# Group 3's queries and keys turned by the crossbar, with the output weights loaded behind two groups' rows

## The chip, the core and the metric

The kernel runs on one core of a Trainium2 chip. The metric is the time of one execution on the device in microseconds, as the median of several runs. The core has five engines with queues of their own: TensorE (PE, matrix products; PEld is its weight load), VectorE (DVE), ScalarE (ACT), GpSimd (POOL) and SyncE (SP). Here POOL issues all loads that change the type from float32 to bfloat16, SP issues the crossbar transposes and most stores, and ACT issues a few stores. An engine works through its queue in order, and an instruction that waits holds everything behind it on that engine.

## What is computed

Windowed attention with a few sink positions, and behind it a gated feed-forward block on the joined heads.

```python
B, H, S, D = 4, 8, 768, 64;  n_sink, window = 4, 128
scores = (q @ k.T) / sqrt(D)                  # by batch and head
keep = (col < n_sink) | ((row - col >= 0) & (row - col < window))
a = softmax(where(keep, scores, -1e9))
x = (a @ v).transpose(0, 2, 1, 3).reshape(3072, 512)
g = x @ w_gate                                # 512 x 1536
out = (g * sigmoid(g) * (x @ w_val)) @ w_out  # w_out: 1536 x 512
```

## The kernel before

**Groups and blocks.** Attention goes by groups of 256 tokens, three to a batch: group 0 to 2 are batch 0, group 3 to 5 batch 1, and so on to group 11. The feed-forward block goes by token blocks of `SIZES` = 256, 256, 256, 512, 512, 512, 512, 256. Block 3 takes groups 3 and 4, block 4 groups 5 and 6.

**The steps of a group.** `load_nat` (L106) loads the group's rows of k and q, four loads of 128 KB, into a tile `nat`. The rows must be turned, so that the head's dimension lies across the partitions: the tiles `kT` and `qT`. There are two ways. `step_TN` (L273) turns 128 tokens of k or q with four PE transposes into one PSUM bank (`pn`, L279), and ACT or DVE copies the bank out (L283, L285). `xbar` (L287) has SP issue four crossbar transposes (L293), straight from `nat` into `kT` and `qT`. Before the change group 2 and group 3 go by `step_TN`, and groups 4 to 11 by `xbar`. Then come:

- `step_S1`, `step_S2`, `step_S3`: the scores on PE (L382), the exponentials on ACT (L395), and the products with the mask on DVE (L404). `step_S1` also takes the scores of the sinks (`mm_K`, L432).
- `step_PV` (L469): the product with v on PE (L454 and L463 for sinks and neighbours, L494), and the division by the sum on DVE (L503, L511) into `xn`.
- `step_X` (L523): `xn` is turned into the feed-forward input `xT`, for groups above 2 by two crossbar transposes on SP (L538).

`load_v` loads v, for the first group of a batch as `va` (L151), for the others as parts of `vm` (L128).

**The feed-forward steps.** A gate unit (`gate`) makes one PSUM bank each of x times `w_gate` (`pg`) and x times `w_val` (`pv`), both at L564, with a tanh on ACT (L584) and two DVE operations (L592 and L598 to L607) into `ht`. An output unit (`down`, L644) multiplies 128 tokens of `ht` with the four tiles `wo` of the output weights, twelve matmuls of 512 columns (L657), copies the bank out on ACT (L662) and stores it (L665). Three matmuls use each tile `wo`.

**The order.** It is written out by hand. The list `us` holds the units of the feed-forward block, and `weave` runs them in turn; `slots` gives each unit the attention steps that are put into it. In the first list, units 0 to 3 belong to blocks 0 and 1, units 4 to 11 to both, units 12 to 17 are the gate units of block 2, and units 18 to 23 are six output units, two for each of the blocks 0, 1 and 2. In an output unit the steps are spread evenly between its twelve matmuls:

```python
for i, a in enumerate(attn):
    at.setdefault(DFC * (i + 1) // (len(attn) + 1), []).append(a)
```

A step marked `ahead` runs before a gate unit's first product. In the second list block 3 starts, whose first two units need the turned results of group 3 and whose next two those of group 4; group 5's scores stand in its second unit.

**The loads.** Before the first list, POOL's queue gets all weights and the rows and v of groups 2 and 3 in the order of the code: gate weights 1 and 2, rows of group 2, gate weights 3, v of group 2, gate weights 4 and 5, four output weights (`load_out`), rows of group 3, v of group 3. Rows and v of group 4 follow. POOL's loads take turns on eight semaphores, and each load waits until the load eight places before it has landed. SP's and ACT's transfers share eight others in the same way. `vcl` holds the sinks' v of batches 1 to 3: POOL clears it, and SP loads eight small pieces into it.

**Buffers.** The pool `rowp` has three buffers under the tag `rows`: two first hold the staged rows of group 0, one those of group 1, and then `nat` of groups 2 and 3 take one each. From group 4 on `nat` has one buffer of its own in `natp`, so that the rows of a group wait for the transposes of the group before. PSUM has eight banks for everything (`bank`).

Of the kernel before, what the change touches and what calls it, by code (L numbers as in the profile page):

```python
# [8 lines left out]
BF16 = mybir.dt.bfloat16  # L9
# [5 lines left out]
def kernel(  # L15
# [12 lines left out]
    nc = tc.nc  # L28
    P = 128
# [3 lines left out]
    DM = moe_w_gate.shape[0]  # L33
# [21 lines left out]
    def pool(name, bufs, psum=False):  # L55
        if psum:
            return ctx.enter_context(
                tc.tile_pool(name=name, bufs=bufs, space=bass.MemoryType.PSUM))
        return ctx.enter_context(tc.tile_pool(name=name, bufs=bufs))

    const = pool("const", 1)
    wpool = pool("wpool", 1)
    rowp = pool("rowp", 3)
    natp = pool("natp", 1)
# [19 lines left out]
    rows, nats, vas = {}, {}, {}  # L84
# [20 lines left out]

    def load_nat(g):  # L106
        b, c = divmod(g, GC)
        x = (natp if g > 3 else rowp).tile(
            [P, 2, 2, DM], BF16, tag="nat" if g > 3 else "rows", name="nat")
        for i, src in ((0, k), (1, q)):  # L110
            for j in range(2):
                t0 = c * 256 + j * P
                nc.gpsimd.dma_start(  # L113
                    x[:, i, j].rearrange("p (h d) -> p h d", d=D),
                    src[b, :, t0:t0 + P].rearrange("h p d -> p h d"))
        nats[g] = x
# [3 lines left out]
    def load_vm(g):  # L120

        b, c = divmod(g, GC)
        if b not in vms:
            vms[b] = vpool.tile([P, 6, H, VS], BF16, tag=f"vm{b}", name="vm")
            nc.gpsimd.memset(vms[b][:, :, :, D:D + 1], 1.0)

        def part(t, p0, p1, t0):
            nc.gpsimd.dma_start(  # L128
                vms[b][p0:p1, t - 1, :, 0:D],
                v[b, :, t0:t0 + p1 - p0].rearrange("h p d -> p h d"))  # L130

        T = 2 * c
        if g - 1 not in QG:
            part(T - 1, 0, 64, P * (T - 1))
            part(T, 0, P, P * T - 64)
        part(T + 1, 0, 64, P * (T + 1))
        part(T + 1, 64, P, P * (T + 1) - 64)
        if c == GC - 1:
            part(T + 2, 0, 64, P * (T + 2) - 64)
        else:  # L140
            part(T + 2, 0, P, P * (T + 2) - 64)

    def load_v(g):
        if g in QG:
            return load_vm(g)
        b, c = divmod(g, GC)
        va = vpool.tile([P, 2, H, VS], BF16, tag=f"va{g}", name="va")
        nc.vector.memset(va[:, :, :, D:D + 1], 1.0)
        for j in range(2):
            t0 = c * 256 + j * P  # L150
            nc.gpsimd.dma_start(  # L151
                va[:, j, :, 0:D], v[b, :, t0:t0 + P].rearrange("h p d -> p h d"))
        vas[g] = va

    wgs, wvs, wos = [], [], []

    def load_gate(i, which=(0, 1)):
        f0, n = sum(FCH[:i]) * P, FCH[i] * P
        both = (wgs, moe_w_gate, "wg"), (wvs, moe_w_val, "wv")
        for lst, w, nm in (both[x] for x in which):  # L160
            t = wpool.tile([P, DMC, n], BF16, tag=f"{nm}{i}", name=nm)
            nc.gpsimd.dma_start(
                t, w[:, f0:f0 + n].rearrange("(c p) f -> p c f", p=P))
            lst.append(t)

    def load_out(i):
        n = DFC // 4
        t = wpool.tile([P, n, DM], BF16, tag=f"wo{i}", name="wo")
        nc.gpsimd.dma_start(
            t, moe_w_out[i * n * P:(i + 1) * n * P].rearrange("(c p) f -> p c f", p=P))  # L170
        wos.append(t)
# [7 lines left out]
    vcl = const.tile([P, B - 1, D + 1], FP32)  # L179
# [3 lines left out]
    zero = const.tile([P, 512], BF16)  # L183
    one = const.tile([P, 1], FP32)
    warmed = const.tile([P, 1], FP32)
    KW = 32
    kss = const.tile([P, B, NP2, KW + 2 * NS], BF16)
    vsbs = []
# [19 lines left out]
    def load_sinks(t, b0, b1):  # L208
        for h in range(H):
            r = 32 * (h // 4) + NS * (h % 4)  # L210
            nc.sync.dma_start(
                t[r:r + NS, :, 0:D], v[b0:b1, h, 0:NS].rearrange("b s d -> s b d"))
# [34 lines left out]
    def new_T(b):  # L247
        if b not in kTs:
            kTs[b] = kqtp.tile([P, NP2, S], BF16, tag="kT", name="kT")
            qTs[b] = kqtp.tile([P, NP2, S], BF16, tag="qT", name="qT")  # L250

    def step_T(g, i, p2, evict=None):
        b, c = divmod(g, GC)
        new_T(b)
        x = rows[g]
        pt = bank([P, 2, 256], FP32, "pt")
        for pp in range(2):
            p = 2 * p2 + pp
            for r in range(4):
                for w in range(2):  # L260
                    h = slice(64 * w, 64 * (w + 1))
                    nc.tensor.matmul(
                        pt[h, pp, 64 * r:64 * (r + 1)], x[h, i, p, r * D:(r + 1) * D],
                        ident[h, h], start=True, stop=True, skip_group_check=True)
        dst = (kTs, qTs)[i][b][:, 2 * p2:2 * p2 + 2, c * 256:(c + 1) * 256].rearrange(
            "q a (m r) -> q a m r", r=4)
        pt = pt.rearrange("q a (r m) -> q a m r", r=4)
        if (evict or ("a", "v")[i]) == "a":
            nc.scalar.copy(out=dst, in_=pt)
        else:  # L270
            nc.vector.tensor_copy(out=dst, in_=pt)
# [15 lines left out]
    def xbar(g, which=(0, 1)):  # L287
        b, c = divmod(g, GC)
        new_T(b)
        for i in which:  # L290
            for j in range(2):
                t0 = c * 256 + j * P
                nc.sync.dma_start_transpose(  # L293
                    (kTs, qTs)[i][b][:, :, t0:t0 + P], nats[g][:, i, j])
# [47 lines left out]
    def build_maskq():  # L342

        nc.gpsimd.memset(maskq, 1.0)
        for up, m, sl in ((0, 0, slice(1, 4, 2)), (0, 1, slice(2, 5, 2)),
                          (1, 0, slice(2, 6, 3)), (1, 1, slice(0, 4, 3))):
            r = slice(64 * up, 64 * (up + 1))
            nc.gpsimd.tensor_copy(
                out=maskq[r, sl],
                in_=mask[r, 0:1, P * m + 64 * up:P * m + 64 * up + 64].broadcast_to(  # L350
                    [64, 2, 64]))
# [70 lines left out]
    def mm_K(g):  # L422
# [3 lines left out]
        for a in range(2):  # L426
            for j in range(2):
                for hh in range(2):
                    r, p = 32 * (2 * j + hh), 2 * hh + a
                    t0 = c * 256 + j * P  # L430
                    k0 = (KW + 2 * NS) * p - 2 * NS * a
                    nc.tensor.matmul(  # L432
                        ps[r:r + KW], kfl[:, b, k0:k0 + KW], qTs[b][:, p, t0:t0 + P],
                        start=(a == 0), stop=(a == 1), skip_group_check=True)
# [238 lines left out]
    def A(fn, *a):  # L673
        return lambda: fn(*a)

    def TN(g, evict="av"):
        return [A(step_TN, g, i, j, evict) for j in range(2) for i in range(2)]
# [4 lines left out]
    def S1(g, apart=False):  # L682
        f = A(step_S1, g, apart)
        f.ahead = True
        return f

    def one(at, g, apart=False):
        return [(at, [S1(g, apart), A(step_S2, g, apart)]), (at + 1, [A(step_S3, g)])]

    def ahead(f):  # L690
        g = lambda: f()
        g.ahead = True
        return g

    def PVs(g):
        return [A(step_PV, g, j, hh) for hh in range(2) for j in range(2)]

    def Xs(g):
        return [A(step_X, g, j) for j in range(2)]
# [104 lines left out]
    load_gate(2)  # L804
    step_vsb(0)
    load_nat(2)
    load_gate(3)
    load_v(2)
    load_gate(4)
    load_gate(5)  # L810
    for i in range(4):
        load_out(i)
    load_nat(3)
    load_v(3)
    nc.gpsimd.memset(vcl, 0.0)
    nc.gpsimd.memset(vcl[:, :, D:D + 1], 1.0)
    load_sinks(vcl, 1, B)
    build_maskq()

    step_T(1, 0, 0, "a")  # L820
    step_T(1, 0, 1, "a")
# [29 lines left out]
    def L(*fs):  # L851
        def f():
            for x in fs:
                x()
        return f

    def NV(g):
        return L(A(load_nat, g), A(load_v, g))
# [2 lines left out]
        (4, TN(2)[::2]), (5, TN(2)[1::2]), ((6, 7), Ss(2)), (6, [K(2)]),  # L861
        ((8, 8), PVs(2)[:2]), (9, [A(step_PV, 2, 0, 1, "a"), A(step_PV, 2, 1, 1, "a")]),
        ((10, 11), [A(step_X, 2, 0, "a"), ahead(A(step_X, 2, 1, "a"))]),
        (11, [NV(4), lambda: nc.gpsimd.tensor_copy(out=vcl[64:128], in_=vcl[0:64])]),
        ((14, 14, 15, 15), TN(3, "aa")),
        (15, [A(xbar, 4)]), (15, [A(load_nat, 5)]), (19, [A(xbar, 5, (0,))]),
        *one(17, 3), (18, [A(step_ks, 1)]), (18, [A(step_vsb, 1)]),
        ((19, 19, 19, 20), PVs(3)), (19, [S1(4)]), (20, [L(A(step_S2, 4), A(step_S3, 4))]), (20, Xs(3)), (20, [A(xbar, 5, (1,))]),
        ((21, 21, 21, 22), PVs(4)), (21, Xs(4)[:1]),
        (22, [Xs(4)[1], flush, A(behind, 3, 511), A(load_v, 5), A(load_nat, 6)]),  # L870
        (23, [A(xbar, 6), A(turned, 6), A(load_v, 6), NV(7)])))

# [52 lines left out]
```

## Time and profile before

| | |
|---|---|
| median of 3 runs | 233.8 us (233.5 to 235.35) |
| the profiled execution | 233.03 us, its span 231.2 us |
| PE | 226.0 us busy (98%) |
| DVE, ACT, POOL | 151.1, 106.3 and 84.8 us busy |
| granted PE clock | 1.00 throughout |
| DMA, 20 to 50 us | share 1.32 to 2.24, 162 to 203 GB/s |
| PE transposes of L279 | 32, of 219 ns each; half of them group 3's |
| the four loads of `wo` | issued from 27.1 to 29.9 us, 9.7 to 12.7 us to landing |
| crossbar transposes of L293 | 32, of some 1.2 us each on SP's queue |

The span runs from the first to the last instruction; the rest of the execution's time lies around it. A DMA share above 1 means that transfers of several queues overlap on the engines, since the time of each packet is counted. In a timeline row the first number is the start, the second the time, then engine, line, operation, tile written and tiles read, and the number of instructions merged; in brackets stands the idle time before it and what ended it. Matmuls are pipelined, so one instruction's duration is longer than the distance to the next: 219 ns stand for one transpose, but eight follow each other in about 0.45 us.

### The profile page before, as it was taken

How to read it: one execution, taken by the hardware profiler on the slowest of the kernel's cores; microseconds unless marked ns; L12 is line 12 of the kernel's file. 1: busy time of each engine (PE TensorE's matmuls, PEld its weight loads, DVE VectorE, ACT ScalarE, POOL GpSimd, SP SyncE). 2: the span in 40 equal slices, each digit the busy share in tenths (PEclk: the TensorE clock that was granted, in tenths of full speed). 3: DMA queues.
4: the chain of work that ended last, by engine and by line, in shares of the span. 5: the costliest groups of instructions: out<-in, count | busy, mean ns of one | idle time of the engine just before them, and what ended most of it. 6: DMA issues, size and time to landing. Idle time of an engine off the chain costs nothing.

```text
span 231.2 us, 5467 instructions
## 1 busy us (share of the span) xinstructions
PE 226.0 (98%) x2171; PEld 126.8 (55%) x2171; DVE 151.1 (65%) x327; ACT 106.3 (46%) x212; POOL 84.8 (37%) x123
## 2 busy tenths in 40 slices
PE   7989999999999999999999999999999999999994
PEld 3669545786556854455454454454454544487443
DVE  5898888767650797960897960697960599778000
ACT  4784496367523827323626412735512823333221
POOL 8997965960500906904526064362000000000000
PEclk9999999999999999999999999999999999999999
DMA  7999999999998998998999999989814102000132
GB/s 134 164 188 178 179 199 206 163 155 125 154 168 211 80 132 103 145 197 124 134 124 118 147 87 203 144 107 131 94 48 136 48 0 45 3 0 0 69 116 91
DMA packets 112008, 28.04 MB, mean 121 GB/s; under 512 B 99056, under 2 KB 109040, under 8 KB 111984
## 3 DMA queue, kind: packets, MB, share of 16 engines
q0 software_dynamic: 79904, 14.29, 80.7%
q1 hardware_dynamic: 30672, 11.58, 28.5%
q10 hardware_dynamic: 1408, 1.84, 2.8%
q8 instruction: 17, 0.28, 0.5%
q14 instruction: 7, 0.06, 0.1%
HBM read 29.13 MB, written 6.29 MB: 153 GB/s over the span
## 4 chain that ended last, share of the span: by engine, by line
PE 93%; DMA 4%; DVE 1%; ACTq 0%; ACT 0%; issue 0%
PE pg L564 27%; PE pv L564 27%; PE pd L657 27%; PE o L494 3%; PE s L382 3%; DMA wg<-in_moe_w_gate_dram 3%; DMA st<-in_q_dram 2%; PE o L463 1%; PE pn L279 1%; PE o L454 1%; PE pk L432 1%; PE s L326 0%; PE px L543 0%; DVE kT L755 0%; PE pt L746 0%; PE s L765 0%
## 5 line engine op out<-in xcount | busy, mean ns | idle before, releaser
L592 DVE SCALAR_TENSOR_TENSOR u<-th,pg 128x512 bf16<-128x512 f32 x72 | 49.1, 683 | 45.3 <-ACT th L584 44.9
L564 PE MATMUL pg<-xT,wg 128*128 128x512 bf16 (+1 forms) x368 | 74.2, 333 | 0.5 <-DMA wg<-in_moe_w_gate_dram 0.5
L564 PE MATMUL pv<-xT,wv 128*128 128x512 bf16 (+1 forms) x368 | 74.1, 333 | 0.0
L584 ACT ACTIVATE th<-pg 128x512 f32<-128x512 f32 x72 | 43.8, 608 | 59.4 <-PE pg L564 59.2
L657 PE MATMUL pd<-wo,ht 128*128 128x512 bf16 (+2 forms) x300 | 65.9, 370 | 0.0
L564 PEld LDWEIGHTS <-wg 128*128 128x128 bf16 x368 | 35.2, 98 | 26.5 <-DMA wg<-in_moe_w_gate_dram 0.7
L564 PEld LDWEIGHTS <-wv 128*128 128x128 bf16 x368 | 34.6, 98 | 22.8 <-issue 0.2
L607 DVE TENSOR_TENSOR ht<-u,pv 128x512 bf16<-128x512 bf16 x60 | 41.2, 686 | 4.5 <-PE pv L564 0.4
L657 PEld LDWEIGHTS <-ht 128*128 128x128 bf16 x300 | 27.6, 98 | 28.4
L662 ACT ACTIVATE ot<-pd 128x512 f32<-128x512 f32 (+1 forms) x24 | 14.3, 595 | 50.2 <-PE pd L657 50.2
L395 ACT ACTIVATE e<-s 128x512 bf16<-128x512 f32 x54 | 28.5, 614 | 5.8 <-PE s L382 5.4
L113 POOL DMA_DIRECT2D nat<-in_k_dram x20 | 17.8, 896 | 28.6 <-DMA qT<-nat 27.1
L511 DVE TENSOR_TENSOR xn<-o,rcp 128x256 bf16<-128x256 f32 x45 | 17.9, 420 | 0.7
L128 POOL DMA_DIRECT2D vm<-in_v_dram x24 | 17.8, 772 | 1.1 <-DMA va<-in_v_dram 0.8
L113 POOL DMA_DIRECT2D nat<-in_q_dram x20 | 17.8, 908 | 1.0 <-DMA wg<-in_moe_w_gate_dram 0.8
L494 PEld LDWEIGHTS <-e 128*128 128x128 bf16 x256 | 11.5, 98 | 6.0 <-issue 0.2
L404 DVE TENSOR_TENSOR e<-e,maskq 128x768 bf16<-128x768 bf16 x24 | 13.1, 552 | 1.9 <-ACT e L395 1.9
L151 POOL DMA_DIRECT2D va<-in_v_dram x12 | 10.7, 921 | 4.5 <-DMA wo<-in_moe_w_out_dram 2.5
L703 POOL CAST warmed<-xT 1x1 f32<-1x1 bf16 x3 | 0.5, 175 | 28.5 <-DMA xT<-xn 28.5
L503 DVE RECIPROCAL rcp<-o 128x4 f32<-128x4 f32 x48 | 7.1, 171 | 4.8 <-PE o L494 4.5
L664 DVE TENSOR_SCALAR ot<-pd 128x128 f32<-128x128 f32 x1 | 0.3, 292 | 14.3 <-PE pd L657 14.3
L333 ACT ACTIVATE e<-s 128x512 bf16<-128x512 f32 x16 | 8.3, 625 | 0.3 <-PE s L326 0.3
(86 smaller groups left out, 141.4 us busy)
## 6 DMA issues: line engine op xcount, KB each, us to landing
out_dram<-ot SPq DMA_DIRECT2D x17, 256.0 KB
nat<-in_k_dram POOLq DMA_DIRECT2D x20, 128.0 KB, 4.2
nat<-in_q_dram POOLq DMA_DIRECT2D x20, 128.0 KB, 5.2
va<-in_v_dram POOLq DMA_DIRECT2D x12, 128.0 KB, 5.5
wg<-in_moe_w_gate_dram POOLq DMA_DIRECT2D x6, 256.0 KB, 7.1
wv<-in_moe_w_val_dram POOLq DMA_DIRECT2D x6, 256.0 KB, 7.6
wo<-in_moe_w_out_dram POOLq DMA_DIRECT2D x4, 384.0 KB, 11.1
out_dram<-ot ACTq DMA_DIRECT2D x6, 256.0 KB
```

The source lines that it names most:

```text
L113: nc.gpsimd.dma_start(x[:, i, j].rearrange("p (h d) -> p h d", d=D), src[b, :, t0:t0 + P].rearrange("h p d -> p h d"))
L128: nc.gpsimd.dma_start(vms[b][p0:p1, t - 1, :, 0:D], v[b, :, t0:t0 + p1 - p0].rearrange("h p d -> p h d"))
L395: nc.scalar.activation(e_t[g][:, e0:e0 + 512], pss[g][w, i], AF.Exp, scale=scale)
L404: nc.vector.tensor_tensor(e, e, m.broadcast_to([P, 2, 384]), op=ALU.mult)
L494: nc.tensor.matmul(o, l, r, start=(c == 0 and i == 0), stop=(i == len(mms) - 1), skip_group_check=True)
L511: nc.vector.tensor_tensor(xn, po[:, :, 0:D], rcp.broadcast_to([P, 4, D]), op=ALU.mult)
L564: nc.tensor.matmul(ps[:, i * n:(i + 1) * n], ws[fi][:, c, fo * P:(fo + 1) * P], xTs[tb][:, c], start=(c == 0), stop=(c == DMC - 1))
L584: nc.scalar.activation(th, pg, AF.Tanh, scale=0.5)
L592: nc.vector.scalar_tensor_tensor(u, th, 1.0, pg, op0=ALU.add, op1=ALU.mult)
L607: nc.vector.tensor_tensor(hts[tb][:, f:f + 512 // SIZES[tb]].rearrange("p a n -> p (a n)"), u, pv, op=ALU.mult)
L657: nc.tensor.matmul(po, hts[tb][:, f, ts * P:(ts + 1) * P], wos[f // n][:, f % n, lo:hi], start=(f == 0), stop=(f == DFC - 1))
L662: nc.scalar.activation(ot, po, AF.Copy, scale=0.5)
```

## The change

- The rows of group 3 and of group 4 are loaded before the output weights, and the clearing of `vcl` and the loads into it stand before them.
- Group 3 is turned by `xbar(3)`, right behind the request for its rows, and its four `step_TN` (units 14 and 15) go.
- `nat` of group 5 takes the third buffer of `rowp`, in place of the single buffer of `natp`.
- SP gets a small copy that reads the last output weight into a new tile `landed`. `xbar(4)`, which stood in unit 15, is issued behind it, ahead of the first list. As SP works in order, group 4's transposes and all later SP work stand behind this copy.
- Group 4's scores, at the end of unit 19 before, stand in the middle of unit 20. Two empty steps (`L()`) make the spreading put them there. Group 3's product with v moves from units 19 and 20 to units 20 and 21, its turned result from 20 to 21, and all four products of group 4 with v and both turned results into unit 22.
- Group 4's v is still loaded in unit 11, its rows no longer.

```diff
     def load_nat(g):
         b, c = divmod(g, GC)
-        x = (natp if g > 3 else rowp).tile(
-            [P, 2, 2, DM], BF16, tag="nat" if g > 3 else "rows", name="nat")
+        x = (natp if g > 3 and g != 5 else rowp).tile(
+            [P, 2, 2, DM], BF16, tag="nat" if g > 3 and g != 5 else "rows", name="nat")
...
     warmed = const.tile([P, 1], FP32)
+    landed = const.tile([1, 64], BF16)
...
     load_gate(5)
-    for i in range(4):
-        load_out(i)
-    load_nat(3)
-    load_v(3)
     nc.gpsimd.memset(vcl, 0.0)
     nc.gpsimd.memset(vcl[:, :, D:D + 1], 1.0)
     load_sinks(vcl, 1, B)
+    load_nat(3)
+    xbar(3)
+    load_nat(4)
+    for i in range(4):
+        load_out(i)
+    load_v(3)
     build_maskq()
+    nc.sync.dma_start(landed, wos[3][0:1, 0, 0:64])
+    xbar(4)
...
-        (11, [NV(4), lambda: nc.gpsimd.tensor_copy(out=vcl[64:128], in_=vcl[0:64])]),
-        ((14, 14, 15, 15), TN(3, "aa")),
-        (15, [A(xbar, 4)]), (15, [A(load_nat, 5)]), (19, [A(xbar, 5, (0,))]),
+        (11, [A(load_v, 4), lambda: nc.gpsimd.tensor_copy(out=vcl[64:128], in_=vcl[0:64])]),
+        (15, [A(load_nat, 5)]), (19, [A(xbar, 5, (0,))]),
         *one(17, 3), (18, [A(step_ks, 1)]), (18, [A(step_vsb, 1)]),
-        ((19, 19, 19, 20), PVs(3)), (19, [S1(4)]), (20, [L(A(step_S2, 4), A(step_S3, 4))]), (20, Xs(3)), (20, [A(xbar, 5, (1,))]),
-        ((21, 21, 21, 22), PVs(4)), (21, Xs(4)[:1]),
+        (20, [L(), L(), S1(4), L(A(step_S2, 4), A(step_S3, 4))]),
+        ((20, 21, 21, 21), PVs(3)), (21, Xs(3)), (21, [A(xbar, 5, (1,))]),
+        ((22, 22, 22, 22), PVs(4)), (22, Xs(4)[:1]),
         (22, [Xs(4)[1], flush, A(behind, 3, 511), A(load_v, 5), A(load_nat, 6)]),
```

## The prediction

> **What bounds the kernel now.** I read the page first: the engines' shares, the chain, then the timeline of TensorE (PE), of GpSimd's load queue (POOL) and of SyncE's queue (SP) from 20 to 90 us.
>
> ```profile
> PE 226.0 (98%) x2171; PEld 126.8 (55%) x2171; DVE 151.1 (65%) x327; ACT 106.3 (46%) x212; POOL 84.8 (37%) x123
> ...
> PE 93%; DMA 4%; DVE 1%; ACTq 0%; ACT 0%; issue 0%
> ```
>
> PE is busy for 226.0 of 231.2 us and carries 93% of the chain that sets the end. From 20 us on it never stops for long, so the time falls only by work taken off PE and rises by every us that PE waits in its order. ACT's share is 46%: what is taken off ACT alone is worth nothing.
>
> ```profile
> 46.24 0.61 PE L279 MATMUL pn<-ident,nat 128*128 128x128 bf16 x8
> 46.69 1.04 PE L564 MATMUL pv<-xT,wv 128*128 128x256 bf16 x8
> ...
> 48.44 0.61 PE L279 MATMUL pn<-ident,nat 128*128 128x128 bf16 x8
> 48.88 1.04 PE L564 MATMUL pv<-xT,wv 128*128 128x256 bf16 x8
> ...
> 54.13 3.62 PE L657 MATMUL pd<-wo,ht 128*128 128x512 bf16 x16
> ...
> 59.45 0.89 PE L382 MATMUL s<-qT,kT 64*64 64x192 bf16 x52
> ...
> 60.51 1.04 PE L657 MATMUL pd<-wo,ht 128*128 128x512 bf16 x4
> ```
>
> The reader is to see what is removed (two bursts of eight transposes), when the output weights are first used (54.13), and when group 4's scores are taken (59.45).
>
> ```profile
> 31.23 0.91 POOL L113 DMA_DIRECT2D nat<-in_k_dram  x1 [0.54 <-DMA wg<-in_moe_w_gate_dram]
> ...
> 39.48 0.88 POOL L151 DMA_DIRECT2D va<-in_v_dram  x1 [1.47 <-DMA wo<-in_moe_w_out_dram]
> ...
> 48.98 1.69 POOL L128 DMA_DIRECT2D vm<-in_v_dram  x2 [0.78 <-DMA va<-in_v_dram]
> ...
> 57.27 1.75 POOL L113 DMA_DIRECT2D nat<-in_k_dram  x2 [6.22 <-DMA qT<-nat]
> ```
>
> POOL's queue is full here: each load waits until the load eight places before it has landed. So these rows date landings. The row at 57.27 dates the end of group 4's four crossbar transposes.
>
> ```profile
> 49.52 2.58 SPq L293 DMA_TRANSPOSE kT<-nat  x2
> 52.20 2.52 SPq L293 DMA_TRANSPOSE qT<-nat  x2
> ```
>
> ```profile
> 42.00:44.00 2.00, 2.00 (x21) 1.80 (x19) 1.70 (x3) 0.60 (x1) 2.00 (x5) 1.00 2.40 155
> ...
> 56.00:58.00 2.00, 2.00 (x15) 0.99 (x13) 1.96 (x7) 0.60 (x1) 0.73 (x1) 1.00 0.08 12
> ```
>
> In the table by stretches (last two columns: DMA share, GB/s) the DMA engines are loaded to 56 us and empty from 56 to 58. Today, then, the weights and group 4's transposes come in time, with some us to spare. The change spends that spare time.
>
> **The change, part by part.**
>
> 1. Removed: group 3's 16 PE transposes. Each burst delays the projection behind it by 0.45 us (46.24 to 46.69) and 0.44 us (48.44 to 48.88): 0.89 us off PE, all of it on the chain. Their four evictions on ACT (0.6 us each) go too, at no gain, since ACT is not the bound.
>
> 2. Added on SP: four crossbar transposes for group 3. Its rows are now requested right behind the gate weights, at about 27.6 us, and land from about 36 us; the transposes are done by about 46. Their reader, group 3's scores at 51.60 now and about 50.7 after, is covered. On SP only the small sink loads stand before them, issued at about 28 us in place of 40.65, as the memset of 0.38 us that they need moves ahead of these rows on POOL too.
>
> The Trainium skill's page "VectorE: DVE Perf Modes", section "The three transpose paths", prices a 128x128 transpose at 390 ns on TensorE and 1309 ns by the crossbar, and prefers TensorE: a rule against this change. By it group 3's sixteen blocks would take 20.9 us from 36, to 57, and group 3's scores would wait some 6 us (an estimate from that page). The trace, 7.75 us for the same sixteen blocks of group 4 and 0.055 us a block on PE, does not agree, and is used.
>
> 3. Moved: the four output-weight loads, now behind eight row loads of 128 KB (groups 3 and 4). The last gate weight lands at about 35.3 us (waits end at 31.23, 32.55 and 34.20; one step more). Eight row loads cost 8 x 0.85 = 6.8 us at the 155 GB/s of the row above, or 8 x 1.06 = 8.5 us by landings (the last output weight, issued at 29.9, lands 12.7 us later at 42.6 by the tile's longest time to landing; from there to 48.95 six loads of this size land, 1.06 us each). The weights themselves take 42.6 - 35.3 = 7.3 us. Group 3's transposes run beside them. What this costs the loads no row shows directly; the nearest is the stretch after 49.52: 832 KB of loads were left, 5.5 us at 155 GB/s, so 55.0, and traffic ended at about 56.0. So at least 1.0 us; at most half of the 5.1 us that four issues take, 2.6 us. A gain is excluded: bytes are only added. I take 1.6, nearer the measured stretch. The last output weight then lands at 35.3 + 6.8 + 7.3 + 1.0 = 50.4 to 35.3 + 8.5 + 7.3 + 2.6 = 53.7; I take 52.0. PE starts the first output product at 54.13 - 0.89 = 53.24 and needs the last quarter nine matmuls of 0.216 us later, at 55.2. No wait, with 1.5 us to spare at the worst end; later than that, each us is a us. Group 3's v follows the weights, landing at about 54 (PE needs it at 61.6), and group 4's v by about 58 (needed at 65.9).
>
> 4. The new wait: a tiny copy on SP that reads the last output weight. SP stands there until about 52.0, and group 4's transposes behind it start at 52.3 (bounds 50.7 to 54.0) where they start at 49.52 now. Behind them on SP stand group 5's key transposes and the transposes of group 3's and 4's results. ACT's stores share semaphores with SP: the second waits for the copy, the third and fourth for transposes. They are due at 59 us and later, and I cost them at nothing: a held store delays only the next eviction, and a product of 12 matmuls, 2.6 us, hides it. Without that cover a product's bank would come free late, a us for each us.
>
> 5. Group 4's scores move from the end of the second output product to the middle of the third: 53.24 + 30 x 0.216 = 59.7 us, against 59.45 now. They need all four transposes. Now these take 57.27 - 49.52 = 7.75 us from first issue to last landing. Elsewhere it was 7.0 (81.40 to 88.44) and 10.1 (123.22 to 133.36). After the change more loads are still to come in this stretch (256 KB of v, 448 KB of v, and 512 KB of group 5's rows, 1,216 KB against 832), so I take 8.0. Landing: 52.3 + 8.0 = 60.3; PE waits 60.3 - 59.7 = 0.6 us. The ends: 50.7 + 7.0 = 57.7, no wait; 54.0 + 10.1 = 64.1, 4.4 us.
>
> The Trainium skill's page "DMA: Bandwidth & Descriptors", section "Queues, rings and completion order", says that each DMA engine alternates between the queues that have work, packet by packet. By that rule loads could lose half their rate while transposes are in flight, and the sum would move to the 2.6 us end of step 3 (weights at 53.0, a wait of 1.6 us). The stretch from 49.52 to 56.0, 1.0 us, does not bear out so much.
>
> 6. What follows. Group 3's attention products, four of them, move behind these scores, and their normalisations on DVE queue behind group 4's four masks (0.55 us each). With the scores at time s, the masks end at about s + 4.3, the normalisations (0.66 us each, from the rows at 57.92 and 58.58) at s + 6.8. Group 3's result transposes are issued at about s + 6.2 and s + 7.5; by the 2.8 to 3.9 us that such ones take (71.28 plus 1.25 to 75.32; 61.98 to 65.83, where a store was held by the landing) they land by s + 11.4. PE needs them at s + 12.0. Group 5's scores need theirs at s + 13.8, landed by 13.9, and group 4's result at s + 16.7, landed by 16.4. All cost nothing or 0.1 us, but with about 0.5 us to spare where there were 2 us. Group 5's rows no longer wait for group 4's transposes (a buffer of their own), so they land by about 63 us, before s + 6.2 asks for SP.
>
> **Sum.** -0.89 + 0.6 = -0.3 us. Against the profiled execution's 233.03 us (span 231.2, 1.83 around it): 232.7. That execution lies 0.77 below the median of the runs, 233.8, so the median becomes 233.5. One per cent, about what a measurement of this kernel can tell from no change, is 2.3 us.
>
> **Rivals.**
>
> No wait (chance 0.28). The transposes land by 59.7 us: the weights at 51.5 and 7.75 us suffice. For it: the value of now. Against it: the heavier traffic. Time: 233.8 - 0.9 = 232.9.
>
> Group 4's transposes late (0.24), the other side. Place: the weights before the scores in the middle of the third output product. It decides from a landing of 60.6 us (59.7 + 0.9): beyond that each us is a us lost. With the weights at 53.5 and the 10.1 us seen at 123.22, the landing is 63.9, the wait 4.2 and the net +3.3: 237.1. With 9.0 us from 53.0 the net is +1.7: 235.5. For it: DMA is full to 56 us already, and four transposes of 128 KB are added ahead. Against: 10.1 us was seen where output stores stood among SP's transposes.
>
> The wait moves on (0.06): the scores come in time, but the results' transposes take 5.1 us (the last of the four at 123.22, issued at 128.2, landed at 133.36). Then group 3's result is 0.6 us late, group 5's transposes 0.6 more, and the next 0.3: net about +0.6, 234.4. Little speaks for it, as DMA is light after 66 us (share 0.95 at 68 to 70).
>
> The change doesn't do what it says (0.02): if the weights land before SP reaches the copy, nothing is held, and group 4's transposes run beside the weights; the time is that of no wait, 232.9.
>
> **How the numbers follow.** The forecast, a wait of 0.1 to 1.7 us, has 0.40 and its own range is 233.0 to 234.6. Its times and the no-wait, moved-on and not-held cases all lie within 2.3 us of 233.8; of the late case's 0.24 about 0.15 lies beyond +2.3. Faster by over 1% is out of reach of a gain of 0.89 and is left for the scatter of medians (233.5 to 235.35 were seen): 0.03. So 0.03, 0.82, 0.15. Predicted 233.5; low 232.5 is no wait less 0.4 of scatter, high 236.4 takes in most of the late case.
>
> **What would show it.** Right: no transposes of `nat` on PE after 30 us; POOL's output-weight loads issued from about 36 us; the first output product at about 53.2 without a DMA wait; SP's copy at about 52; PE idle of 0 to 1.7 us before L383 at about 60. Wrong: PE idle before L658 on `wo` (step 3), PE idle over 2 us before L383 (step 5), or before L565 at 72 to 77 us (step 6).

## The result

| | before | after |
|---|---|---|
| median of 6 runs | 234.54 us (233.5 to 235.46) | 239.64 us (238.2 to 241.76) |
| ratio | | 1.026, 95% interval 1.022 to 1.030 |
| the profiled execution, its span | 233.03, 231.2 | 239.61, 237.8 |

The change makes the kernel 2.6% slower, some 6 us. Ratios are worked out over the runs in the chip's faster state and are not quotients of the medians (239.64 / 234.54 is 1.022); what a kernel costs in us is taken from its ratio below too. The prediction was 233.5 us, in a range of 232.5 to 236.4. From the page of the kernel after, the engines' shares and the chain:

```profile
PE 226.2 (95%) x2129; PEld 127.8 (54%) x2155; DVE 150.3 (63%) x327; ACT 104.6 (44%) x208; POOL 84.9 (36%) x123
...
PE 59%; DMA 22%; POOL 6%; DVE 4%; SPq 4%; issue 3%; ACTq 0%; ACT 0%; DVEq 0%; POOLq 0%
```

PE's busy time did not fall although 16 transposes are gone, because other matmuls ran slower, and DMA now has 22% of the chain, where it had 4%. Where PE waits, its timeline shows:

```profile
50.41 1.04 PE L565 MATMUL pv<-xT,wv 128*128 128x256 bf16 x8
54.93 1.46 PE L383 MATMUL s<-qT,kT 64*128 64x256 bf16 x18 [3.48 <-DMA qT<-nat]
56.32 1.89 PE L565 MATMUL pg<-xT,wg 128*128 128x256 bf16 x8
58.01 1.11 PE L565 MATMUL pv<-xT,wv 128*128 128x256 bf16 x8
58.95 6.64 PE L658 MATMUL pd<-wo,ht 128*128 128x512 bf16 x29
66.62 0.89 PE L383 MATMUL s<-qT,kT 64*64 64x192 bf16 x52 [1.03 <-DMA qT<-nat]
...
78.67 1.04 PE L565 MATMUL pg<-xT,wg 128*128 128x256 bf16 x8
```

In the kernel before the same places were, without a wait:

```profile
51.60 0.84 PE L382 MATMUL s<-qT,kT 64*128 64x256 bf16 x18
52.37 1.05 PE L564 MATMUL pg<-xT,wg 128*128 128x256 bf16 x8
...
72.75 1.04 PE L564 MATMUL pg<-xT,wg 128*128 128x256 bf16 x8
```

The two bursts of `pn` are gone. The large wait is not at group 4's scores (66.62, 1.03 us), which the prediction had watched, but at group 3's (54.93, 3.48 us), which it had called covered. The matmuls behind that wait are slow as well (18 score matmuls take 1.46 us in place of 0.84; eight of `pg` 1.89 in place of 1.05). The second list starts at 78.67 instead of 72.75. The account of these 5.92 us: +0.68 that is there before any changed work, at the first gate product (15.77 against 15.09, scatter between executions), -0.83 for the transposes (from there to group 3's scores PE needs 35.68 us in place of 36.51), +3.48 of wait, +1.5 of slow matmuls, +1.1 from there to the second list, most of it the wait at group 4's scores. The end is 6.6 us later than before; 0.42 us of the rest is a wait at group 6's scores (95.57).

The table by stretches (PEclk, DMA share and GB/s are the last three columns) explains the slow matmuls:

```profile
42.00:44.00 2.00, 2.00 (x18) 1.50 (x17) 1.45 (x3) 0.92 (x2) 1.84 (x7) 1.00 1.43 156
52.00:54.00 2.00, 0.00 (x0) 0.00 (x0) 0.69 (x1) 0.00 (x0) 0.45 (x1) 1.00 1.91 164
54.00:56.00 2.00, 1.07 (x16) 1.01 (x18) 0.00 (x0) 0.45 (x1) 0.77 (x2) 0.68 2.94 145
56.00:58.00 2.00, 2.00 (x14) 1.21 (x10) 0.00 (x0) 1.12 (x3) 1.66 (x2) 0.50 3.02 147
58.00:60.00 2.00, 1.95 (x13) 1.32 (x13) 1.12 (x3) 1.75 (x4) 1.84 (x3) 0.96 3.25 103
```

After 3.48 us without work the granted clock is 0.68 in one stretch, 0.50 in the next, and back at 0.96 some 4 us after the wait. The Trainium skill's page "TensorE: Matmul & The Clock Gate", Part 1, gives this rule (about 3.4 us idle, then half the clock); the trace of the change agrees. Shorter waits were enough in two other runs: after 2.76 us (e5_tn4) and 2.02 us (e1_wo1024) the granted clock was 0.50 for 3.4 us, while 1.47 us (e2_tn3) left it at 1.00. So 3.4 us is not a safe bound here. The DMA engines, empty from 56 to 58 us before, now move 147 GB/s there.

SP's and POOL's queues date the transfers:

```profile
36.48 2.67 SPq L294 DMA_TRANSPOSE kT<-nat  x2
39.25 2.58 SPq L294 DMA_TRANSPOSE qT<-nat  x2
55.42 0.62 SPq L822 DMA_DIRECT2D landed<-wo  x1
56.13 2.51 SPq L294 DMA_TRANSPOSE kT<-nat  x2
58.74 2.65 SPq L294 DMA_TRANSPOSE qT<-nat  x2
```

```profile
36.75 0.74 POOL L169 DMA_DIRECT2D wo<-in_moe_w_out_dram  x1
...
39.55 0.77 POOL L169 DMA_DIRECT2D wo<-in_moe_w_out_dram  x1 [0.17 <-issue]
...
48.19 0.69 POOL L128 DMA_DIRECT2D vm<-in_v_dram  x1 [2.13 <-DMA wo<-in_moe_w_out_dram]
51.07 0.68 POOL L128 DMA_DIRECT2D vm<-in_v_dram  x1 [2.19 <-DMA wo<-in_moe_w_out_dram]
53.55 0.88 POOL L128 DMA_DIRECT2D vm<-in_v_dram  x1 [1.80 <-DMA wo<-in_moe_w_out_dram]
```

Group 3's transposes are issued at 36.48 to 40.61, as predicted, and by the landing events of the trace they land at 43.6, 47.7, 51.7 and 54.8. The output weights, issued right beside them, land at 47.9, 50.8, 53.3 and 55.4, so the copy on SP is released at 55.42. Group 4's transposes follow and land by 66.5, 10.4 us after their first issue.

What happened in between is in the DMA view, here of 44 to 48 us (packets, MB, share of 16 engines; q0 carries POOL's loads, q1 what SP issues):

```profile
q0 software_dynamic: 601, 0.59, 89.5%
q1 hardware_dynamic: 599, 0.15, 32.4%
```

601 packets against 599: the two queues take turns packet by packet. A packet of the weights has 1,024 B, one of a transpose 256 B, so the transposes get one fifth of the bytes, 37 GB/s, and 512 KB take 14 us. In the kernel before, the DMA view of 55 to 56 us shows what they do alone:

```profile
q1 hardware_dynamic: 1115, 0.27, 131.0%
```

That is 269 GB/s, 2 us for the same four. Its share of 131% with one queue alone also shows that packets of one queue overlap, so a DMA share above 1 needn't mean several queues.

### The profile page after: what moved, and what is told of

Same layout as the page of the kernel before. It is cut to its first block, busy times and chain, and to the rows that moved or that the text cites. A ratio compares the mean times of both kernels' runs of the same rounds, so it can differ in the third digit from the quotient of the medians.

```text
span 237.8 us, 5414 instructions
## 1 busy us (share of the span) xinstructions
PE 226.2 (95%) x2129; PEld 127.8 (54%) x2155; DVE 150.3 (63%) x327; ACT 104.6 (44%) x208; POOL 84.9 (36%) x123
## 4 chain that ended last, share of the span: by engine, by line
PE 59%; DMA 22%; POOL 6%; DVE 4%; SPq 4%; issue 3%; ACTq 0%; ACT 0%; DVEq 0%; POOLq 0%
PE pd L658 20%; PE pg L565 16%; PE pv L565 16%; DMA va<-in_v_dram 7%; DMA wv<-in_moe_w_val_dram 4%; DMA qT<-nat 4%; DMA wg<-in_moe_w_gate_dram 3%; SPq L294 3%; PE s L383 2%; PE o L495 2%; DMA nat<-in_k_dram 2%; DMA st<-in_q_dram 2%; POOL wo L169 1%; DMA xT<-xn 1%; POOL nat L113 1%
## 5 line engine op out<-in xcount | busy, mean ns | idle before, releaser
L658 PE MATMUL pd<-wo,ht 128*128 128x512 bf16 (+2 forms) x289 | 64.4, 370 | 0.6 <-issue 0.2
L565 PEld LDWEIGHTS <-wg 128*128 128x128 bf16 x368 | 35.7, 99 | 26.5 <-issue 0.8
L396 ACT ACTIVATE e<-s 128x512 bf16<-128x512 f32 x54 | 28.4, 614 | 9.3 <-PE s L383 9.3
L495 PEld LDWEIGHTS <-e 128*128 128x128 bf16 x256 | 11.9, 100 | 5.8 <-issue 0.3
L383 PE MATMUL s<-qT,kT 64*64 64x64 bf16 (+4 forms) x366 | 8.5, 223 | 4.9 <-DMA qT<-nat 4.9
L383 PEld LDWEIGHTS <-kT 64*64 64x64 bf16 (+1 forms) x366 | 6.8, 108 | 8.5 <-issue 8.4
```

The lines of the kernel that those rows point to most:

```text
L383: nc.tensor.matmul(pss[g][w, lo // 8][part, 64 * (lo % 8):64 * (lo % 8) + 64 * (hi - lo)], kTs[b][r, p, k0:k0 + kn], qTs[b][r, p, cc:cc + ...
L396: nc.scalar.activation(e_t[g][:, e0:e0 + 512], pss[g][w, i], AF.Exp, scale=scale)
L495: nc.tensor.matmul(o, l, r, start=(c == 0 and i == 0), stop=(i == len(mms) - 1), skip_group_check=True)
L565: nc.tensor.matmul(ps[:, i * n:(i + 1) * n], ws[fi][:, c, fo * P:(fo + 1) * P], xTs[tb][:, c], start=(c == 0), stop=(c == DMC - 1))
L658: nc.tensor.matmul(po, hts[tb][:, f, ts * P:(ts + 1) * P], wos[f // n][:, f % n, lo:hi], start=(f == 0), stop=(f == DFC - 1))
```

## The experiments

The theory (A in the texts on record): the transposes share each DMA engine by packet, so they end only when the weights do, which is after group 3's deadline. Its rivals: it is the number of bytes, the order of the loads, the held copy, the new order of the products, or the crossbar itself. The kernel before, run again beside each set, had medians of 233.41 (the four rows behind the change), 233.43 (the next four) and 233.6 us (the last four). "Lands" is read from the landing events.

| kernel | group 3 by | held copy | rows ahead | new order of products | median us | ratio (95%) |
|---|---|---|---|---|---|---|
| the change | crossbar | yes | yes | yes | 239.64 | 1.026 (1.022 to 1.030) |
| e1_wo128 | crossbar | yes | yes | yes | 245.38 | 1.054 (1.048 to 1.059) |
| e1_wo1024 | crossbar | yes | yes | yes | 242.52 | 1.035 (1.027 to 1.043) |
| e2_tn3 | PE | yes | yes | yes | 237.28 | 1.015 (1.009 to 1.021) |
| e3_nohold | crossbar | no | yes | yes | 239.27 | 1.026 (1.022 to 1.030) |
| e5_tn4 | crossbar (4 on PE) | no | yes | yes | 238.78 | 1.021 (1.016 to 1.025) |
| e6_early | crossbar, earlier | no | yes | yes | 239.46 | 1.024 (1.020 to 1.028) |
| e4_fill | crossbar | yes | yes | yes | 243.25 | 1.042 (1.039 to 1.046) |
| e7_fill_nohold | crossbar | no | yes | yes | 239.42 | 1.026 (1.020 to 1.031) |
| e8_rows | PE | no | yes | no | 233.32 | 0.999 (0.997 to 1.001) |
| e10_order | PE | no | no | yes | 235.01 | 1.005 (1.003 to 1.008) |
| e9_swap | crossbar | no | no | no | 242.63 | 1.040 (1.036 to 1.044) |
| e11_plain | PE (+ plain copies) | yes | yes | yes | 240.73 | 1.034 (1.028 to 1.040) |

**The size of the weights' packets.** Twelve loads of 128 KB in place of four of 384 KB, into a tile whose rows are cut into pieces of 64 columns, and the same twelve loads uncut as a control:

```diff
-        t = wpool.tile([P, n, DM], BF16, tag=f"wo{i}", name="wo")
-        nc.gpsimd.dma_start(
-            t, moe_w_out[i * n * P:(i + 1) * n * P].rearrange("(c p) f -> p c f", p=P))
+        t = wpool.tile([P, n, 8, 64 + 8], BF16, tag=f"wo{i}", name="wo")
+        for c in range(n):
+            nc.gpsimd.dma_start(
+                t[:, c, :, 0:64],
+                moe_w_out[(i * n + c) * P:(i * n + c + 1) * P].rearrange(
+                    "p (a x) -> p a x", x=64))
...
-                    po, hts[tb][:, f, ts * P:(ts + 1) * P], wos[f // n][:, f % n, lo:hi],
+                    po, hts[tb][:, f, ts * P:(ts + 1) * P],
+                    wos[f // n][:, f % n, lo // 64:hi // 64, 0:64],
```

> The output weights come as twelve loads of 128 KB into a padded tile, so that their DMA packets are 128 bytes in place of 1,024. Theory A (shares by packet: the DMA engines take one packet of the transposes, 256 bytes, for one of the loads, whatever its size): beside the weights the transposes now get two thirds of the traffic in place of a fifth; group 3's four transposes land by about 48 us in place of 54.8 and PE does not wait for them. The weights take longer (1.5 MB at some 155 GB/s, 10 us in place of 7.3), land at 55 to 57 us, and group 4's transposes land at 65 to 67 as now, so the whole wait moves to group 4's scores: 237 to 240 us. Theory B (place in the queue: the transposes finish when the loads queued ahead have landed, whatever the packets): group 3's transposes land at 54 to 56 us and PE waits 3 to 5 us at group 3's scores, as now.

> The control of the kernel before it: twelve loads of 128 KB, but with packets of 1,024 bytes as now. Theory A: as the changed kernel, group 3's transposes land at 54 to 56 us, PE waits 3 to 4 us at group 3's scores, 238 to 241 us. Theory B: the same. If the number of loads and not the packet is what counts, it goes with the kernel of 128-byte packets.

With 128 B packets group 3's transposes landed at 48.1 us, with 1,024 B at 52.9 (first issues at 36 to 37 in both), and PE's wait at group 3's scores was gone in the first and 2.02 us in the second. The small packets did what the theory said; the control fell short of its 54 to 56 us and its wait of 3 to 4. The turns were not one to one with the small packets, though: from 44 to 46 us in e1_wo128 the DMA view has

```profile
q0 software_dynamic: 1275, 0.16, 128.7%
q1 hardware_dynamic: 554, 0.13, 60.8%
```

2.3 load packets to one of a transpose, which still gives the transposes 65 GB/s in place of 37. In the control they were not one to one either: from 44 to 48 us its DMA view counts 600 load packets and 850 of the transposes. Why the number of loads changes the turns isn't shown. The totals lay above the expected ranges, by 5.4 us with the small packets and by 1.5 in the control. With the small packets the weights came at 57.0 us, behind them the copy and group 4's transposes, which took 13 us:

```profile
57.05 4.26 PE L661 MATMUL pd<-wo,ht 128*128 128x512 bf16 x19 [0.41 <-DMA wo<-in_moe_w_out_dram]
70.81 1.49 PE L386 MATMUL s<-qT,kT 64*64 64x192 bf16 x50 [9.50 <-DMA qT<-nat]
```

So there are two deadlines in a row, and here more is lost at the second than is gained at the first. The control too waited longer there, 3.92 us.

**Group 3 on PE again, and the copy left out.**

```diff
# e2_tn3
-    xbar(3)
+        ((14, 14, 15, 15), TN(3, "aa")),
# e3_nohold
-    nc.sync.dma_start(landed, wos[3][0:1, 0, 0:64])
```

> Group 3 is turned on PE again in units 14 and 15; everything else of the change stays (order of the loads, hold, places). Theory A: with nothing beside them the weights land at 50 to 52 us, the held transposes of group 4 start by 52.5 and land at 60 to 62, against scores that PE reaches at about 61.3 (59.7, plus 0.9 for the PE transposes, plus 0.7 that this profile is later from its start): PE waits 0 to 1 us, 234 to 236 us. If the hold alone were the loss (group 4's transposes at 66.5 whatever stands before), PE would wait 5 us there and the time would stay at 239 to 240.

> The copy that waits for the last output weight is left out, so that group 4's transposes follow group 3's on SP at about 42 us. Theory A: eight transposes then run beside the weights, one landing each 3 to 4 us while packets of 1,024 bytes run; group 3's land at 54 to 56 as now (wait of 3.5 us), group 4's at 61 to 64, before PE asks for them at about 65.6. The wait of 1 us there goes and the weights land 1 to 2 us later, at 56 to 58: 238 to 240 us. A rival, that the hold is what protects the weights: without it they land after 60 us and PE waits over 2 us at the first output product, 240 to 243 us.

Without group 3's transposes beside them the weights landed at 49.97 us, 5.4 us earlier than in the change. Group 4's transposes still took 11.9 us (50.71 to 62.65), and PE waited 1.47 us for them, more than the expected 0 to 1; the time was 1.48% above before, 237.28 against the expected 234 to 236. Without the copy the weights landed at 55.44, no later than with it (55.4): beside group 3's transposes it protects nothing. Group 4's scores then didn't wait, group 3's waited 4.39 us, and the total stayed. PE's timelines, e2_tn3 and then e3_nohold:

```profile
62.90 0.89 PE L383 MATMUL s<-qT,kT 64*64 64x192 bf16 x52 [1.47 <-DMA qT<-nat]
```

```profile
55.40 1.46 PE L382 MATMUL s<-qT,kT 64*128 64x256 bf16 x18 [4.39 <-DMA qT<-nat]
```

**Is it the bytes? Group 4 on PE, and group 3's transposes earlier.**

```diff
# e5_tn4
-    nc.sync.dma_start(landed, wos[3][0:1, 0, 0:64])
-    xbar(4)
+        ((14, 14, 15, 15), TN(4, "aa")),
# e6_early
-    load_gate(5)
...
     load_nat(3)
     xbar(3)
+    load_gate(5)
     load_nat(4)
+    xbar(4)
...
-    nc.sync.dma_start(landed, wos[3][0:1, 0, 0:64])
-    xbar(4)
```

> The changed kernel with group 4 turned on PE again (the slots that group 3 had in the kernel before), and so without the held copy and without group 4's crossbar transposes: only group 3's four crossbar transposes are left, beside the output weights. DMA traffic in bytes is that of the kernel before. Theory A (a DMA engine serves the load queue and the transposes packet by packet, so beside packets of 1,024 B the transposes get a fifth of the bytes and end with the weights): group 3's transposes still land at 53 to 55 us, the last output weight too; PE reaches group 3's scores 0.9 us later than in the changed kernel, at about 52.3, and still waits 1.5 to 2.9 us there, then runs 1 to 1.5 us slower; no wait before group 4's scores. Total 236.5 to 238. Rival B (the stretch simply has 512 KB too many to move before 56 us, whichever they are): with these bytes gone both sets come early, group 3's transposes by 51, no wait; 233.4, like the kernel before.

> The changed kernel with group 3's rows loaded one step earlier (ahead of the last two gate loads), and both groups' transposes issued on SP as soon as their rows land, without the held copy: group 3's transposes then run beside loads of 128 B and 512 B packets instead of beside the output weights. Bytes as in the changed kernel. Theory A: group 3's transposes land by 44 to 47, no wait at its scores; the last gate weight lands at about 39, needed at 39 to 40, a wait of 0 to 1 us there; group 4's transposes run beside the weights, issued by 48 to 50, and land at 56 to 60.5, a wait of 0 to 1 us; the last output weight at 54 to 55.5. Total 232.7 to 235. Rival B (the bytes are too many for the stretch, in any order): something of that stretch is late by 3 us or more still, the weights or group 4's transposes; 236 to 239.

e5_tn4 moves as many bytes as the kernel before, yet group 3's transposes landed at 54.6 us and the last weight at 55.3, and PE's timeline has

```profile
54.72 1.47 PE L382 MATMUL s<-qT,kT 64*128 64x256 bf16 x18 [2.76 <-DMA qT<-nat]
```

So the loss is there without more bytes; the total was 0.8 us above the expected 238. In e6_early, with the bytes of the change, the theory failed as a guide, and the rival that counts bytes came nearer (it expected the weights or group 4's transposes late by 3 us or more and 236 to 239 us; the measured 239.46 came with the last weight at 61.5 in place of 54 to 55.5): more bytes may add to the loss. Issued from 33.89 us, beside small packets at first, group 3's transposes landed at 42.4, 46.2, 50.8 and 54.0, not by 47: the last three ran beside the weights after all. And the weights came later than ever, at 61.5 us:

```profile
54.12 0.84 PE L382 MATMUL s<-qT,kT 64*128 64x256 bf16 x18 [1.04 <-DMA qT<-nat]
59.02 0.81 PE L657 MATMUL pd<-wo,ht 128*128 128x512 bf16 x3 [0.91 <-DMA wo<-in_moe_w_out_dram]
61.53 6.28 PE L657 MATMUL pd<-wo,ht 128*128 128x512 bf16 x21 [1.71 <-DMA wo<-in_moe_w_out_dram]
```

The first of these waits would have been longer but for a late start: in this execution the granted clock was 0.50 from 17 to 20 us, and PE came to these scores at 53.08, 1.6 us later than in the change (51.45). Here a second effect is seen in the landing events. The trace has sixteen of them for each load, as many as there are DMA engines, but doesn't say which engine one is from. For the last row load of group 4 nine came at 42.5 to 43.1 and the other seven at 46.8 to 51.8, and each weight behind it came in two such groups. That single engines fall behind with transposes in flight and stay behind is the likely reading, and not shown. For the first weight in the change:

```
44.4 44.4 44.5 44.5 44.6 44.6 44.7 44.9 44.9 45.0 45.1 45.2 45.7 45.8 47.8 47.9
```

Two of sixteen parts are 2 us late, and a reader waits for the last. In the kernel before the last weight's parts lie within 1.3 us (41.33 to 42.63). In e2_tn3, where no transposes run beside the weights, they lie within 2.3 us (47.66 to 49.97), but no part is that far behind the one before it.

**The clock.** Sixteen matmuls on zeros in front of group 3's scores, with and without the copy:

```diff
+        (17, [ahead(lambda: fill(16, bank([P, 512], FP32, "w"), 512))]),
         *one(17, 3), (18, [A(step_ks, 1)]), (18, [A(step_vsb, 1)]),
```

> The changed kernel with 16 more matmuls of 512 columns on zeros (a product that nothing reads) just before group 3's scores, about 3.5 us of PE work in place of the idle time there. Theory A with two waits in a row: the granted clock stays at 1.00 after the wait (0.68 and 0.50 in the changed kernel) and the 1.5 us lost there are saved, but group 4's transposes land at 66.5 whatever PE does, so the wait before group 4's scores grows from 1.0 to about 2.5 us: total within 0.7 us of the changed kernel, 239 to 240. Rival (the clock after the wait is a cost of its own that adds to the rest): 238.0.

> The same 16 matmuls in the kernel without the held copy, where group 4's scores didn't wait and group 3's waited 4.4 us (239.3 measured). Theory A: with no second wait behind it, the saved clock is kept: 237.4 to 238.3. Rival (the slower records after the wait cost nothing that lasts, or the clock falls anyway): 239.3, as without the matmuls.

The clock stayed at 1.00 in e7_fill_nohold from 54 to 60 us (0.50 without the matmuls), and its second list starts 2.0 us earlier (76.80 against 78.83). Yet the median, 239.42, is that of e3_nohold, 239.27, as the rival said, and the intervals reach 1.0 to 1.3 us to each side: a gain that lasts isn't shown. In its profile the lead shrinks to 0.7 us at the end of the span, in part by waits of 0.80 us for group 6's transposes (94.08) and 0.56 for transposed results (150.23). With the copy, e4_fill, it was 3.6 us slower than the change, which neither side expected: group 4's transposes landed at about 68.3, 1.8 us later than in the change, and PE waited 4.98 us for them. Why these took 12.9 us and not 10.4 stays open.

**The parts of the change one at a time.** e8_rows is the kernel before with its loads in the new order, e10_order the kernel before with only the new order of the products, e9_swap the kernel before with only this:

```diff
     load_sinks(vcl, 1, B)
+    xbar(3)
...
-        ((14, 14, 15, 15), TN(3, "aa")),
```

> The kernel before with only its loads reordered as in the change (group 3's and 4's rows and the sinks ahead of the output weights, a buffer of its own for group 5): group 3 still turned on PE, products in the old order, no held copy. Group 4's four crossbar transposes are issued as soon as its rows are in (about 42 to 50 us) and run beside the output weights, as group 3's did in the changed kernel. Theory A (the loss in the changed kernel is the deadline of group 3's transposes, which group 4's don't have): they land at about 55, needed at 59.45; the last output weight at about 55, needed at 56: no wait over 0.5 us, 233.0 to 234.5. Rival B (the reordering of the loads itself costs: the weights, or what stands behind them, come too late): a wait on wo of 1 us or more, or on v or group 5's rows; 235 to 237.

> The kernel before with only the job list of the change (group 4's scores one product later, group 3's and 4's attention products and result transposes behind them); loads, transposes on PE and the crossbar as before. The prediction's step 6 says that this order costs nothing: 233.0 to 234.0, no wait from 60 to 105 us. Rival (the results' transposes come later on SP, and with them group 5's and 6's rows and scores, which is why in the kernel with group 3 back on PE 2.2 us of lateness at the start of the second list had grown to 5.7 us at its output products): waits of 1 to 3 us at 75 to 95 us, 235 to 237.

> The kernel before with only group 3's transposes moved from PE to the crossbar: loads and products in the old order (output weights first). Group 3's rows land at 43.5 to 46.3 us, its transposes run beside loads of 128 B packets, where the kernel with small packets showed 1.3 to 2 us for each: they land at 50 to 52, needed at 50.7. Group 4's transposes, issued at about 50 to 53, land at 57 to 59. Theory A: a wait of 0 to 1.5 us at group 3's scores, 0 to 0.5 at group 4's, 0.9 us saved: 232.7 to 234.5. Rival (a transpose in flight holds up the loads whatever their packets, by engines that stand still for 2 to 3 us): rows and v of both groups land 2 to 4 us later, waits of 2 us and more at group 3's or 4's scores: 235 to 238.

e8_rows costs nothing (0.999). Its four transposes, group 4's, run beside the weights as group 3's do in the change, and take nearly as long, 14.6 us, from 40.35 to 54.96; but they are needed only at 60.3. SP's queue and PE's timeline:

```profile
40.35 2.62 SPq L293 DMA_TRANSPOSE kT<-nat  x2
43.06 3.07 SPq L293 DMA_TRANSPOSE qT<-nat  x2
```

```profile
52.46 0.84 PE L382 MATMUL s<-qT,kT 64*128 64x256 bf16 x18
...
54.98 3.62 PE L657 MATMUL pd<-wo,ht 128*128 128x512 bf16 x16
...
60.31 0.89 PE L382 MATMUL s<-qT,kT 64*64 64x192 bf16 x52
```

No bracket stands behind any of them. The same slow transfer is free where its reader comes 20 us after the first issue, and costs a wait of 3.5 us where it comes after 15 (36.48 to 51.45, in the change). The new order of the products costs 0.5%, 1.2 us; the expectation of no cost was wrong. The profile has it in one wait, at group 6's scores, for DVE:

```profile
91.28 0.84 PE L382 MATMUL s<-qT,kT 64*128 64x256 bf16 x18 [1.37 <-DVE ht L607]
```

And e9_swap, a bare exchange of 0.9 us of PE for four crossbar transposes, costs 4.0%, 9.2 us. Issued at 45.79, they land at 53.3, 55.0, 56.2 and 57.5:

```profile
57.66 1.47 PE L382 MATMUL s<-qT,kT 64*128 64x256 bf16 x18 [6.64 <-DMA qT<-nat]
```

Here they run beside row loads with packets of 128 B, at 1,271 load packets to 553 from 52 to 54 us. So small packets alone don't save them: the last lands 11.7 us after the first issue, and the first of them only after 7.5 us. The expected 50 to 52 was wrong, and the rival right on the wait, though not on the size (its 238 is 4.6 us short), and its reason, engines that stand still, isn't shown here.

**The crossbar or the second queue?** Group 3 on PE, and four plain copies of its rows on SP in the place of the transposes, to a tile that nothing reads:

```diff
-    xbar(3)
+    for i in range(2):
+        for j in range(2):
+            nc.sync.dma_start(
+                aside[:, i, j, :, 0:96],
+                nats[3][:, i, j].rearrange("p (a x) -> p a x", x=128)[:, :, 0:96])
```

> The changed kernel with group 3 turned on PE, and in the place of its crossbar transposes four plain copies on SP of its rows to a tile that nothing reads, in as many packets (2,048, of 192 B against the transposes' 256 B): the same queue beside the output weights, without the crossbar. Theory A (what costs is the sharing by packet): the copies also last until 52 to 55 us, and the last output weight lands at 54 to 55.5 in place of 50.0. Rival (it is the crossbar that is slow beside loads and makes single engines fall behind): the copies are done by 46 to 49, the sixteen parts of a weight's landing lie within 1.5 us of each other (3.5 us in the changed kernel), and the last output weight lands by 51.5 to 52.5. The time is not what this run is for: 237 to 240.

The copies landed at 43.5, 47.3, 51.6 and 53.7, the last weight at 53.9 (49.97 without the copies). The DMA view of 44 to 48 us:

```profile
q0 software_dynamic: 646, 0.62, 92.3%
q1 hardware_dynamic: 657, 0.12, 27.9%
```

Plain copies take the same turns, last nearly as long (16.3 us from the first issue; 18.3 for the transposes) and hold the weights up by 4 us, of which 1 us is a later issue of the weights (37.72 against 36.74). One part came 2.5 us behind the others here too (47.4 against 44.9 for the first weight). So sharing between two queues does this without the crossbar. The crossbar's transposes held the weights up by 5.4 us; whether the difference is the crossbar or their larger packets (256 B against 192) stays open. The time of this run, 240.73, holds a wait of 5.81 us at group 4's scores.

Taken together, the runs show that the late transposes of group 3 make the wait (it is gone with them on PE in e2_tn3, and there with them alone in e9_swap), and that sharing DMA engines with loads makes them late. How the turns are dealt is shown for the loads of the change, and open for 128 B packets and for loads of 128 KB.

## Why the prediction was wrong

- **Step 2 failed, and the forecast with it.** "Done by about 46" is 54.8, so "covered" became a wait of 3.48 us and 1.5 us of slow clock. The 7.75 us for the same four in the kernel before were not a price in company: issued at 49.52 to 53.5, beside loads, they landed at 55.1 to 56.7 (7.2 us by the landing events), and about half of their packets ran from 55 to 56, with no load beside them (the row of 1,115 packets above). The duration dated the end of the loads. In company the same four took 11.7 us (e9_swap), 11.9 (e2_tn3), 14.6 (e8_rows) and 18.3 (the change).
- **The Trainium skill's rule was weighed the wrong way round.** In step 3 the alternation of the Trainium skill's page "DMA: Bandwidth & Descriptors", section "Queues, rings and completion order", was used for what the loads lose. The trace agrees with the rule (601 to 599), but beside larger packets it is the small ones that starve. The rule that spoke against the change, from the Trainium skill's page "VectorE: DVE Perf Modes", gave an end at 57 us and a wait of some 6, and was set aside as too dear; the change measured 54.8 and 3.48, nearer to it than to the forecast of 46 and no wait. It was near by luck, since its price is not what was paid: alone the four take 2 us.
- **Step 3's term was too small.** Last weight at 55.4 in place of 52.0, outside the bounds of 50.4 to 53.7. With group 3 on PE it lands at 49.97, so the transposes cost the loads 5.4 us and not 1.6. Some 1 us of it is two late parts (fourteen of the last weight's parts were there by 54.05, two came at 55.4), which no row of before showed. PE did not wait for the weights, as it was late itself.
- **Step 4** was right in mechanism (SP released when the weights land, 55.42), and the copy costs nothing beside the crossbar for group 3 (e3_nohold, 239.27 without it). Without that crossbar, copy and rows ahead together cost some 2 us (e2_tn3 against e10_order, 237.28 and 235.01); no run tells the two apart in the new order.
- **Step 5's term** of 8.0 us was 10.4, from a start at 56.13 in place of 52.3: landed at 66.5 instead of 60.3. The wait is only 1.03 because PE came 5.9 us late (65.59 in place of 59.7).
- **Step 6** called the new order free; alone it costs 1.2 us (e10_order). That a delay can come back later is also seen in e2_tn3, where 2.2 us at the start of the second list are 5.7 at its output products, in an execution 2 us above that kernel's median.
- **Step 1** held: no `pn` for group 3, 0.83 us saved where 0.89 was forecast.
- None of the rivals named the place. "Group 4's transposes late" had the sign, but gave +3.3 us at most, at the other group.

The costs don't add. The new order alone is +1.2 us; with the copy and rows ahead +3.5; with group 3's crossbar +6; that crossbar alone, in the old order of loads, +9.2. Each wait hides part of the next. None of these kernels beats the one before; e8_rows equals it.

## What to carry to other kernels

A transfer's time from issue to landing in a busy stretch says when the traffic ended, not what the transfer costs; look where its packets ran before using it as a price. Work with small packets put beside large loads can end as late as the loads do (54.8 and 55.4 us here), so give it a deadline after that, or leave it on an engine: 0.9 us on a full PE was cheaper here than 512 KB on a full DMA. Where two late transfers stand in a row, taking one wait away shows little; undo the parts one at a time from the kernel before.

## What was not expected of the hardware

- Two queues on the same DMA engines took turns by packet when the loads had packets of 1,024 B and came in pieces of 384 KB (601 to 599; 646 to 657 for plain copies), but not with 128 B packets, where 2.3 went to one (1,275 to 554; 1,271 to 553), nor with 1,024 B in pieces of 128 KB (600 to 850).
- With two queues busy, some of the sixteen parts of a load came 2 to 9 us behind the first ones, and the last part sets the landing.
- The granted clock fell to 0.50 for 3.4 us after waits of PE of 2.02 and 2.76 us.
- Beside full load queues the first packet of a transpose ran 3.5 us after its issue (36.48 to 40.0); for group 4's, later in the same execution, it was 2.1 us (56.13 to 58.2).
